# Weight-piece operations with a constant as second input, a later copy of the turned reciprocals, and a new order of the attention stage

## The chip, the cores and the metric

The kernel runs on one core of a Trainium2 chip. The core has TensorE (matrix products, PE in the profile, PEld for its weight loads), VectorE (DVE), ScalarE (ACT), GpSimd (POOL) and SyncE (SP, which here only issues DMA transfers). On-chip memory is SBUF, with 128 partitions, and PSUM, into which TensorE writes.

The metric is the device time of one execution in microseconds. The kernel before took 1176.67 us as the median of three runs (1176.46 to 1177.38).

## The reference

Two stages follow one another: attention with a relative position bias for 8 batches, 8 heads, 576 positions and a head size of 64, and then four dense layers on its 4608 output rows of 512 values.

```python
scores = scale * np.matmul(q, k.transpose(0, 1, 3, 2))
rel = (pos[:, None] - pos[None, :])
psi_rel, psi_i = np.log1p(np.abs(rel)), np.log1p(np.maximum(pos[:, None], 1.0))
h = np.maximum((psi_rel / psi_i)[..., None] @ w1 + b1, 0.0)
scores = scores + (h @ w2).transpose(2, 0, 1)[None]
attn = np.exp(scores - np.max(scores, axis=-1, keepdims=True))
attn = attn / (np.sum(attn, axis=-1, keepdims=True) + 1e-09)
x = np.matmul(attn, v)                        # then heads beside one another: 4608 x 512
a, b = x @ moe_w1, x @ moe_w2                 # 512 -> 1024
out = ((a * b) @ moe_w3) @ moe_w_out          # 1024 -> 1024 -> 512
```

The four weight matrices of the dense layers arrive as 64-bit floats.

## The kernel before

**Four parts.** A prologue computes the bias table from w1, b1 and w2 and writes it to DRAM (`nb_d`). The attention stage works through 32 units. Then the product of w3 and w_out is formed (`fold`) while moe_w1 and moe_w2 are converted, and at last 9 chunks of 512 rows pass the dense layers (`up`, `down`).

**A unit** is a pair of heads (4 pairs) and a batch (8 batches); units are numbered u = 8 x pair + batch. A unit's steps have short names, which the tables use:

- `ldq`, `ldk`, `ldv`: loads of q, k and v. `gq`, `gk`: GpSimd splits q and k into a rounded part (qh, kh, L249) and a residue (ql, kl, L250).
- `S0` to `S7`, `SM`: TensorE's score matmuls for nine tiles of query rows (`M` holds the last 64 rows of both heads), L266. Two PSUM buffers, so a score tile waits until the one before the last has been read.
- `T`: VectorE adds the bias to a score tile and takes the row minimum, L277, with one input in PSUM. `E`: ScalarE takes the exponential and the row sums, L302.
- `F0` to `F3`, `FL`, `FN`: TensorE turns the exponentials, L323 to L335; `H`: the copy of such a turned tile out of PSUM (L346 on VectorE, L348 on ScalarE). `W0`, `W1`: the product with v, L386; `X0`, `X1`: its copy out of PSUM; `xd`: its store to DRAM. F, W and R share two PSUM buffers.
- Once per pair, on its last unit: `r` (VectorE adds 1e-9 to the row sums, L307, and takes reciprocals, L308), `R` (TensorE turns them, L318), `HR` (VectorE copies the turned tile, tile name rt), `rd` (16 small stores on SP's queue).

**Weight pieces.** On six units of each pair (batches 1 to 6) one 128x512 piece of w3 or w_out is converted from 64-bit to 32-bit floats by the function `narrow`, in eight steps `c0` to `c7`: load (SP); magnitude of the upper words (ScalarE, L128); lower words to floats (GpSimd, L134); clamp (VectorE, L137); shift (VectorE, L140); sign and top bit (VectorE, L146); exponent mask (VectorE, L151); a product and a sum (GpSimd, L154 and L155). The same function later converts the pieces of moe_w1 and moe_w2, with the third step on ScalarE.

**The order** is written out by hand. `ORDER` holds for each engine the planned start of each step of a unit; unit u's step has the time u x `PERIOD` + the table's value. `arrange` makes this list, and `drive` issues the instructions on TensorE, ScalarE, VectorE and GpSimd in the order of these times. On each engine instructions run strictly in that order, so only the order that the times make counts on the chip, not the times themselves. A time beyond one period means that the step runs one or two periods after its unit began; taken modulo the period, the times give the cyclic order in the steady state. `AT_R` places R, and HR and rd by offsets to it. The load `c0` is placed 4.4 ahead of the first of c1 and c2. `t_s` (last S or E) and `end` (last step) place the parts behind the attention stage.

Of the kernel before, what the change touches and what calls it, by code (L numbers as in the profile page):

```python
# [9 lines left out]
F32 = mybir.dt.float32  # L10
F32R = mybir.dt.float32r
I32 = mybir.dt.int32
U32 = mybir.dt.uint32
AF = mybir.ActivationFunctionType
ALU = mybir.AluOpType
# [3 lines left out]
P = 128  # L19
# [9 lines left out]
AT_W = 3.5, 0.0, 0.5, 1.2, 2.6, 3.8, 5.5, 7.1, 10.0, 10.6  # L29


PERIOD = 12.49
ORDER = {
    "PE": {
        "S0": 0.00, "S3": 0.41, "S1": 1.76, "S7": 2.29, "S5": 4.20, "S2": 7.21, "SM": 7.62, "S6": 9.04, "F1": 13.82,
        "F0": 15.23, "S4": 15.85, "FL": 21.04, "F2": 25.88, "F3": 28.79, "W0": 29.67, "FN": 32.16, "W1": 34.51,
    },
    "DVE": {
        "T0": 0.71, "T3": 1.40, "T1": 2.43, "T7": 3.12, "T5": 6.30, "T2": 7.88, "c3": 9.03, "c4": 9.54, "TM": 10.13,
        "T6": 10.82, "c5": 11.51, "c6": 12.36, "T4": 18.14, "H3": 29.51, "X0": 32.41, "HN": 33.63, "X1": 37.84,  # L40
    },
    "ACT": {
        "E0": 4.39, "E3": 5.18, "E1": 5.97, "c1": 7.61, "E5": 8.21, "E7": 9.29, "E2": 11.03, "E6": 11.82, "EM": 12.61,
        "H1": 15.02, "H0": 15.97, "E4": 19.29, "HL": 22.61, "H2": 26.60,
    },
    "POOL": {
        "gk": -8.54, "gq": -6.29, "c2": 10.54, "c7": 12.84,
    },
    "SP": {"ldk": -18.63, "ldq": -14.18, "ldv": 0.74},
}  # L50
AT_R = 22.64
TILES = "01234567M"
NPP, NTS, NPS = 7, 4, 2

# [1 line left out]
def arrange(NU, pieces):  # L56

    at = {n: (t, e) for e, steps in ORDER.items() for n, t in steps.items()}
    at.update(r=(max(at["E" + t][0] for t in TILES) + 1.0, "DVE"), R=(AT_R, "PE"), HR=(AT_R + 0.85, "DVE"), rd=(AT_R + 1.3, "SP"))
    at["xd"] = max(t for n, (t, _) in at.items() if n[0] == "X") + 0.8, "SP"  # L60
    at["c0"] = min(at["c1"][0], at["c2"][0]) - 4.4, "SP"
    return {(n, u): (u * PERIOD + t if u or n not in FIRST else FIRST[n], e) for u in range(NU) for n, (t, e) in at.items() if (n[0] != "c" or u in pieces) and (n not in ("r", "R", "HR", "rd") or u % 8 == 7)}


@with_exitstack
def relpos_attention_moe(
# [17 lines left out]
    nc = tc.nc  # L84
# [4 lines left out]
    NTOK, DO = out.shape  # L89
# [7 lines left out]
    def f(ap):  # L97
        return ap.bitcast(F32)

    const = ctx.enter_context(tc.tile_pool(name="const", bufs=1))  # L100
    dram = ctx.enter_context(tc.tile_pool(name="dram", bufs=1, space=DRAM))
    ident = const.tile([P, P], F32, name="ident")
    make_identity(nc, ident)


    WIDE = moe_w1.dtype == mybir.dt.int64
    LEAST = struct.unpack("<f", struct.pack("<I", 0x38000000))[0]
    MOST = struct.unpack("<f", struct.pack("<I", 0x47EFFFFF))[0]

    def narrow(pool, src, n, x, queue, pieces=1, low=nc.scalar):  # L110

        d = {}

        def cut(ap):
            return ap if pieces == 1 else ap.rearrange("p (c n) -> p c n", c=pieces)

        def fetch():
            if not WIDE:
                queue.dma_start(cut(x), src)
                return  # L120
            wi = pool.tile([P, n, 2], I32, name="wi")
            flat = wi.rearrange("p n t -> p (n t)")
            queue.dma_start(cut(flat), src.bitcast(I32))
            mag = pool.tile([P, n], F32, name="wmag")
            d.update(lo=wi[:, :, 0], hi=wi[:, :, 1], mag=mag, bits=mag.bitcast(I32), power=flat[:, 0:n])

        def size():
            nc.scalar.activation(d["mag"], f(d["hi"]), AF.Abs)  # L128

        def rest():  # L130
            if low is nc.scalar:
                nc.scalar.activation(x, d["lo"].bitcast(U32), AF.Copy, scale=2.0 ** -52)
            else:
                low.tensor_scalar(x, d["lo"].bitcast(U32), 2.0 ** -52, 1.0, op0=ALU.mult, op1=ALU.mult)  # L134

        def clamp():
            nc.vector.tensor_scalar(d["mag"], d["mag"], LEAST, MOST, op0=ALU.max, op1=ALU.min)  # L137

        def shift():
            nc.vector.tensor_scalar(  # L140
                d["bits"], d["bits"], 3, 0x3FFFFFFF, op0=ALU.logical_shift_left, op1=ALU.bitwise_and,
            )

        def head():

            nc.vector.scalar_tensor_tensor(  # L146
                d["bits"], d["hi"], -0x40000000, d["bits"], op0=ALU.bitwise_and, op1=ALU.bitwise_or,
            )

        def power():  # L150
            nc.vector.tensor_scalar(d["power"], d["bits"], -0x800000, None, op0=ALU.bitwise_and)  # L151

        def total():
            nc.gpsimd.tensor_tensor(x, x, f(d["power"]), op=ALU.mult)  # L154
            nc.gpsimd.tensor_tensor(x, d["mag"], x, op=ALU.add)  # L155

        steps = [fetch, size, rest, clamp, shift, head, power, total]
        return steps if WIDE else [fetch] + [lambda: None] * 7

# [17 lines left out]
    w3s = [[held.tile([P, DF // 2], F32, name=f"w3s{t}{hf}") for hf in range(2)] for t in range(NF)]  # L177
    wos = [held.tile([P, DO], F32, name=f"wos{t}") for t in range(NF)]
# [14 lines left out]
    cva = att_r.enter_context(tc.tile_pool(name="cva", bufs=1, side="right"))  # L193
# [207 lines left out]

    def piece_of(i):
        if i < NF:
            return narrow(cva, moe_w_out[i * P:(i + 1) * P, :], DO, wos[i], nc.sync, low=nc.gpsimd)
        hf, t = divmod(i - NF, NF)
        return narrow(cva, moe_w3[t * P:(t + 1) * P, hf * 512:(hf + 1) * 512], 512, w3s[t][hf], nc.sync, low=nc.gpsimd)

    pieces = dict(zip([u for u in range(NU) if 0 < u % B < B - 1], (piece_of(i) for i in range(3 * NF))))
    assert len(pieces) == 3 * NF

# [5 lines left out]
    for (n, u), (at, on) in arrange(NU, pieces).items():  # L416
        if n[0] == "H":
            step = lambda n=n, u=u, on=on: op_H(u, n[1:], on)
        elif n[0] == "X":
            step = lambda n=n, u=u, on=on: op_X(u, n[1:], on)  # L420
        else:
            step = lambda n=n, u=u: made[n[0]](u, n[1:])
        later.append((at, len(later), step, n, u))
# [8 lines left out]
    with ExitStack() as pro:  # L432
# [29 lines left out]
        def reach(G):  # L462

            return (G + 1) * GR - 1, S - 1 - G * GR
# [9 lines left out]
        for G in range(NGRP):  # L474
            n = max(reach(G)) + 1
# [49 lines left out]
        for G in range(NGRP):  # L525
            at = -LEAD + G * PACE_B
# [36 lines left out]
    def split_w(pool, t, m):  # L563
        src = (moe_w1, moe_w2)[m].rearrange("(c p) n -> p c n", p=P)[:, :, t * P:(t + 1) * P]
        w = cv.tile([P, NC * P], F32, name="w", bufs=3)
        for step in narrow(cv, src, NC * P, w, nc.sync, pieces=NC):
            step()
            yield
        w = w.rearrange("p (c n) -> p c n", c=NC)
        wh = pool.tile([P, NC, P], F32R, name=f"wh{m}{t}")  # L570
        nc.scalar.activation(wh, w, AF.Copy)
        yield
        wl = pool.tile([P, NC, P], F32R, name=f"wl{m}{t}")
        nc.vector.tensor_tensor(wl, w, f(wh), op=ALU.subtract)  # L574
        ups[m, t] = (wh, wl)
# [142 lines left out]
    for n in range(4, 2 * NF):  # L718
        at = t_s + AT_W1 + PACE_W * n
# [91 lines left out]
```

## Time and profile before

| | |
|---|---|
| median of three runs | 1176.67 us |
| profiled execution, its own time | 1171.91 us |
| profiled execution, span | 1170.1 us |
| busy in the span: TensorE, VectorE, ScalarE, GpSimd | 95%, 55%, 47%, 31% |
| mean granted TensorE clock | 0.987 |
| clamp L137, shift L140, mask L151 (40 of each): busy | 52.3, 34.7, 17.3 us |
| L146 (40): busy | 28.5 us |
| score addition T, L277 (288): busy | 207.5 us |

A profile comes from one execution, which need not lie at the median of the others. Times in the timeline are microseconds from the start of the span. A row of the timeline gives start, length, engine, line, operation, tile written and tiles read, shapes, and in brackets the idle time of the engine before it with what ended it. The attention stage takes roughly the stretch from 72 to 505 us, the dense layers alone that from 632 us on.

### The profile page before, as it was taken

What the parts mean: (1) busy time and instruction counts of PE and PEld (TensorE: products, weight loads), DVE (VectorE), ACT (ScalarE), POOL (GpSimd) and SP (SyncE); (2) the same over time, 40 slices, a digit from 0 to 9 for tenths busy, and PEclk for the clock granted to TensorE, in tenths of its full rate; (3) what the DMA queues carried; (4) which work ended last, traced back from release to release, by engine and by line L of the source; (5) the groups of instructions that cost most, each with busy time, mean ns of one, the idle gap of its engine ahead of it and who ended that gap; (6) DMA issues with size and microseconds to landing.
All of it is one profiled execution on the core that took longest, in us unless ns stands there. A gap on an engine that the chain in (4) does not pass through costs nothing.

```text
span 1170.1 us, 22602 instructions
## 1 busy us (share of the span) xinstructions
PE 1111.9 (95%) x9092; PEld 870.1 (74%) x9092; DVE 647.2 (55%) x1296; ACT 551.9 (47%) x1087; POOL 366.5 (31%) x286
## 2 busy tenths in 40 slices
PE   7669998998999999999999999999999999999998
PEld 3147777777777777766787888888888888888887
DVE  8748878888888788849985322213131322213111
ACT  6667887888888788864343212121211212121211
POOL 0446665775567467525453000000000000000000
PEclk9889999999999999999999999999999999999999
DMA  6864474557454645315341211111110211100001
GB/s 204 271 184 138 154 221 136 170 161 220 130 165 146 209 127 164 108 48 179 130 129 52 75 34 60 48 46 63 37 55 18 79 29 64 45 37 1 36 1 36
DMA packets 61512, 123.14 MB, mean 105 GB/s; under 512 B 9696, under 2 KB 19296, under 8 KB 61408
## 3 DMA queue, kind: packets, MB, share of 16 engines
q1 hardware_dynamic: 60112, 120.21, 32.7%
q10 hardware_dynamic: 1296, 1.49, 0.4%
q8 instruction: 71, 1.16, 0.4%
q14 instruction: 33, 0.27, 0.1%
HBM read 91.76 MB, written 29.92 MB: 104 GB/s over the span
## 4 chain that ended last, share of the span: by engine, by line
PE 51%; DVE 5%; ACT 3%; DMA 3%; POOL 1%; issue 1%; ACTq 0%; SPq 0%; DVEq 0%; POOLq 0%
PE up L653 30%; PE o L678 15%; DMA wi<-in_moe_w_dram 3%; PE pst L386 2%; PE s L266 2%; DVE wmag L137 1%; DVE ts L277 1%; PE pst L323 1%; POOL w L154 1%; PE wacc L611 1%; ACT pp L302 1%; DVE w3l L604 1%; ACT wmag L128 0%; DVE wmag L140 0%; ACT ppM L302 0%
## 5 line engine op out<-in xcount | busy, mean ns | idle before, releaser
L661 DVE TENSOR_TENSOR g<-up,a 128x512 f32<-128x512 f32 x72 | 49.7, 690 | 332.2 <-PE up L653 332.2
L277 DVE CUSTOM_DVE_ANT_0 ts<-s,nb 128x576 f32<-128x576 f32 x288 | 207.5, 753 | 41.8 <-PE s L266 27.2
L653 PE MATMUL up<-xh,wh 128*128 128x512 f32 x576 | 225.2, 391 | 0.5 <-POOL xh L639 0.5
L653 PE MATMUL up<-xh,wl 128*128 128x512 f32 x576 | 225.2, 391 | 0.1
L653 PE MATMUL up<-xl,wh 128*128 128x512 f32 x576 | 225.1, 391 | 0.0
L302 ACT ACTIVATE pp<-ts,mx 128x576 f32<-128x576 f32 x256 | 195.9, 768 | 56.5 <-DVE mx L277 52.0
L678 PE MATMUL o<-w3s,gh 128*128 128x512 f32 x576 | 177.8, 390 | 0.3 <-ACT gh L664 0.3
L386 PE MATMUL pst<-pt,rv 128*64 128x256 f32 (+1 forms) x1280 | 169.2, 410 | 0.2 <-ACT pt L348 0.2
L639 POOL TENSOR_SCALAR xh<-xr 128x512 fp32r<-128x512 f32 x36 | 24.1, 671 | 434.6 <-DVE xr L635 434.6
L658 ACT COPY a<-up 128x512 f32<-128x512 f32 x72 | 42.2, 585 | 246.9 <-PE up L653 246.9
L348 ACT ACTIVATE pt<-pst 128x1024 f32<-128x1024 f32 x128 | 126.3, 1013 | 34.5 <-PE pst L323 34.5
L266 PE MATMUL s<-kh,qh 64*128 64x288 f32 x640 | 119.9, 370 | 22.5 <-DVE mx L277 18.9
L386 PEld LDWEIGHTS pst<-pt,rv 128*64 128x64 f32 x1280 | 88.1, 137 | 62.4 <-issue 11.5
L664 ACT ACTIVATE gh<-g 128x512 fp32r<-128x512 f32 x72 | 45.5, 632 | 174.1 <-DVE g L661 174.1
L653 PEld LDWEIGHTS up<-xh,wh 128*128 128x128 f32 x576 | 108.2, 188 | 24.2 <-POOL xh L639 0.9
L653 PEld LDWEIGHTS up<-xh,wl 128*128 128x128 f32 x576 | 108.2, 188 | 23.9 <-DVE wl L574 0.5
L653 PEld LDWEIGHTS up<-xl,wh 128*128 128x128 f32 x576 | 108.2, 188 | 23.3
L678 PEld LDWEIGHTS o<-w3s,gh 128*128 128x128 f32 x576 | 108.0, 188 | 23.5 <-ACT gh L664 0.7
L323 PE MATMUL pst<-ident,pp 64*128 64x64 f32 x2304 | 104.9, 224 | 11.1 <-ACT ppM L302 10.7
L678 PE MATMUL o<-w3s,gl 128*128 128x512 f32 x288 | 112.2, 390 | 0.9 <-DVE gl L667 0.9
L323 PEld LDWEIGHTS pst<-ident,pp 64*128 64x128 f32 x2304 | 98.0, 140 | 14.6 <-issue 8.4
L266 PE MATMUL s<-kh,ql 64*128 64x288 f32 x640 | 96.6, 295 | 2.4 <-POOL ql L250 2.4
(85 smaller groups left out, 1650.1 us busy)
## 6 DMA issues: line engine op xcount, KB each, us to landing
rq<-in_q_dram SPq DMA_DIRECT2D x31, 640.0 KB
wi<-in_moe_w_dram SPq DMA_DIRECT2D x32, 512.0 KB
nb_d<-bev SPq DMA_DIRECT2D x36, 295.5 KB
rv<-in_v_dram SPq DMA_DIRECT2D x32, 320.0 KB
x_d<-x SPq DMA_DIRECT2D x32, 288.0 KB
xr<-x_d SPq DMA_DIRECT2D x36, 256.0 KB
rb<-r_d SPq DMA_DIRECT2D x72, 128.0 KB
rk<-in_k_dram SPq DMA_DIRECT2D x31, 288.0 KB
```

Source lines behind the costliest of these rows:

```text
L266: nc.tensor.matmul(s[:, hf, :HS], Q[x][rows, q0:q0 + P], K[y][rows, h * HS:(h + 1) * HS], start=(m == 0), stop=(m == len(ops) - 1),)
L277: nc.vector.tensor_tensor_reduce(out=halves(ts), in0=d.pop(("s", t))[:, :, :HS], in1=halves(NB[p, t]), op0=ALU.add, op1=ALU.min, scale=-1. ...
L302: nc.scalar.activation(pp, ts, AF.Exp, bias=mx, scale=-1.0, accum_out=sums[p][:, 9 * b + col:9 * b + col + 1])
L323: nc.tensor.transpose(ps[0:n, hf, c0:c0 + 64], x[rows], ident[rows, rows])
L348: nc.scalar.activation(o, x, AF.Copy)
L386: nc.tensor.matmul(o, x[:, c0:c0 + D], m, start=(c == 0), stop=(c == 4 and n_m == len(ms) - 1),)
L639: nc.gpsimd.tensor_scalar(xh, xr, 1.0, 1.0, op0=ALU.mult, op1=ALU.mult)
L653: nc.tensor.matmul(acc, l[:, cc], r, start=(n == 0), stop=(n == 3 * NC - 1))
L658: nc.scalar.copy(a, ps[0])
L661: nc.vector.tensor_tensor(g, ps[1], a, op=ALU.mult)
L664: nc.scalar.activation(gh, g, AF.Copy)
L678: nc.tensor.matmul(d["o", t], l[:, sl], folded[ft][r], start=(ft == 0 and n == 0), stop=(ft == NF - 1 and n == 2),)
```

## The change

1. `narrow` gets an argument `both`. With `both=False` the clamp becomes a two-input operation whose second input is one column (`least`) repeated along the row, and the same holds for the shift (`low30`) and the exponent mask (`top9`). The pieces of w3 and w_out, that is those of the attention stage, use it; those of moe_w1 and moe_w2 keep the old forms. The three columns are filled once at the start.
2. The copy HR of the turned reciprocals has a time of its own, `AT_HR`, 2.05 behind R instead of 0.85; rd follows it by 0.5.
3. `ORDER` and `PERIOD` are new. X1 moves from VectorE to ScalarE, H3 from VectorE to ScalarE and H0 from ScalarE to VectorE; the steps c1 to c7 now lie one period behind their unit's start, gq comes ahead of gk, and the tiles are taken in another sequence.

```diff
-PERIOD = 12.49
+PERIOD = 12.55
 ORDER = {
     "PE": {
-        "S0": 0.00, "S3": 0.41, "S1": 1.76, "S7": 2.29, "S5": 4.20, "S2": 7.21, "SM": 7.62, "S6": 9.04, "F1": 13.82,
-        "F0": 15.23, "S4": 15.85, "FL": 21.04, "F2": 25.88, "F3": 28.79, "W0": 29.67, "FN": 32.16, "W1": 34.51,
+        "S3": 0.00, "S2": 0.64, "S5": 3.54, "S6": 3.95, "S1": 5.36, "S0": 5.79, "SM": 9.39, "F1": 10.28, "S4": 10.75,
+        "S7": 11.63, "F0": 12.08, "F2": 16.91, "FL": 17.38, "FN": 21.83, "F3": 23.71, "W0": 26.15, "W1": 31.30,
     },
     "DVE": {
-        "T0": 0.71, "T3": 1.40, "T1": 2.43, "T7": 3.12, "T5": 6.30, "T2": 7.88, "c3": 9.03, "c4": 9.54, "TM": 10.13,
-        "T6": 10.82, "c5": 11.51, "c6": 12.36, "T4": 18.14, "H3": 29.51, "X0": 32.41, "HN": 33.63, "X1": 37.84,
+        "T3": 0.67, "T2": 1.36, "T5": 4.21, "T6": 4.90, "T1": 7.08, "T0": 9.29, "TM": 10.54, "T4": 11.42, "T7": 12.30,
+        "H0": 14.60, "c3": 18.14, "c4": 18.91, "c5": 20.32, "c6": 21.12, "HN": 22.53, "X0": 28.89,
     },
     "ACT": {
-        "E0": 4.39, "E3": 5.18, "E1": 5.97, "c1": 7.61, "E5": 8.21, "E7": 9.29, "E2": 11.03, "E6": 11.82, "EM": 12.61,
-        "H1": 15.02, "H0": 15.97, "E4": 19.29, "HL": 22.61, "H2": 26.60,
+        "E3": 2.72, "E2": 3.51, "E5": 6.98, "E6": 7.77, "E1": 8.56, "E0": 10.18, "H1": 11.00, "EM": 12.90,
+        "E4": 13.69, "E7": 14.48, "c1": 16.85, "H2": 17.63, "HL": 18.58, "H3": 24.50, "X1": 34.63,
     },
     "POOL": {
-        "gk": -8.54, "gq": -6.29, "c2": 10.54, "c7": 12.84,
+        "gq": -12.80, "gk": -8.50, "c2": 18.85, "c7": 21.92,
     },
-    "SP": {"ldk": -18.63, "ldq": -14.18, "ldv": 0.74},
+    "SP": {"ldk": -18.65, "ldq": -20.75, "ldv": 0.00},
 }
-AT_R = 22.64
+AT_R, AT_HR = 17.63, 19.68
...
-    at.update(..., R=(AT_R, "PE"), HR=(AT_R + 0.85, "DVE"), rd=(AT_R + 1.3, "SP"))
+    at.update(..., R=(AT_R, "PE"), HR=(AT_HR, "DVE"), rd=(AT_HR + 0.5, "SP"))
...
+    least = const.tile([P, 1], F32, name="least")
+    masks = const.tile([P, 2], I32, name="masks")
+    low30, top9 = masks[:, 0:1], masks[:, 1:2]
+    nc.vector.memset(least, struct.unpack("<f", struct.pack("<I", 0x38000000))[0])
+    nc.vector.memset(low30, 0x3FFFFFFF)
+    nc.vector.memset(top9, -0x800000)
...
         def clamp():
-            nc.vector.tensor_scalar(d["mag"], d["mag"], LEAST, MOST, op0=ALU.max, op1=ALU.min)
+            if both:
+                nc.vector.tensor_scalar(d["mag"], d["mag"], LEAST, MOST, op0=ALU.max, op1=ALU.min)
+            else:
+                nc.vector.scalar_tensor_tensor(d["mag"], d["mag"], MOST, least.broadcast_to([P, n]), op0=ALU.min, op1=ALU.max)
...
+                nc.vector.scalar_tensor_tensor(
+                    d["bits"], d["bits"], 3, low30.broadcast_to([P, n]), op0=ALU.logical_shift_left, op1=ALU.bitwise_and,
+                )
...
+                nc.vector.tensor_tensor(d["power"], d["bits"], top9.broadcast_to([P, n]), op=ALU.bitwise_and)
...
-            return narrow(cva, moe_w_out[i * P:(i + 1) * P, :], DO, wos[i], nc.sync, low=nc.gpsimd)
+            return narrow(cva, moe_w_out[i * P:(i + 1) * P, :], DO, wos[i], nc.sync, low=nc.gpsimd, both=False)
```

More of the change, by code (lines that the diff above doesn't have):

```diff
@@ L58, in arrange @@
     at = {n: (t, e) for e, steps in ORDER.items() for n, t in steps.items()}
-    at.update(r=(max(at["E" + t][0] for t in TILES) + 1.0, "DVE"), R=(AT_R, "PE"), HR=(AT_R + 0.85, "DVE"), rd=(AT_R + 1.3, "SP"))
+    at.update(r=(max(at["E" + t][0] for t in TILES) + 1.0, "DVE"), R=(AT_R, "PE"), HR=(AT_HR, "DVE"), rd=(AT_HR + 0.5, "SP"))
     at["xd"] = max(t for n, (t, _) in at.items() if n[0] == "X") + 0.8, "SP"
@@ L108, in relpos_attention_moe, with narrow @@
     MOST = struct.unpack("<f", struct.pack("<I", 0x47EFFFFF))[0]
-    def narrow(pool, src, n, x, queue, pieces=1, low=nc.scalar):
+    def narrow(pool, src, n, x, queue, pieces=1, low=nc.scalar, both=True):
         d = {}
@@ L136, in clamp @@
         def clamp():
-            nc.vector.tensor_scalar(d["mag"], d["mag"], LEAST, MOST, op0=ALU.max, op1=ALU.min)
+            if both:
+                nc.vector.tensor_scalar(d["mag"], d["mag"], LEAST, MOST, op0=ALU.max, op1=ALU.min)
+            else:
+                nc.vector.scalar_tensor_tensor(d["mag"], d["mag"], MOST, least.broadcast_to([P, n]), op0=ALU.min, op1=ALU.max)
         def shift():
-            nc.vector.tensor_scalar(
-                d["bits"], d["bits"], 3, 0x3FFFFFFF, op0=ALU.logical_shift_left, op1=ALU.bitwise_and,
-            )
+            if both:
+                nc.vector.tensor_scalar(
+                    d["bits"], d["bits"], 3, 0x3FFFFFFF, op0=ALU.logical_shift_left, op1=ALU.bitwise_and,
+                )
+            else:
+                nc.vector.scalar_tensor_tensor(
+                    d["bits"], d["bits"], 3, low30.broadcast_to([P, n]), op0=ALU.logical_shift_left, op1=ALU.bitwise_and,
+                )
         def head():
@@ L150, in power @@
         def power():
-            nc.vector.tensor_scalar(d["power"], d["bits"], -0x800000, None, op0=ALU.bitwise_and)
+            if both:
+                nc.vector.tensor_scalar(d["power"], d["bits"], -0x800000, None, op0=ALU.bitwise_and)
+            else:
+                nc.vector.tensor_tensor(d["power"], d["bits"], top9.broadcast_to([P, n]), op=ALU.bitwise_and)
         def total():
@@ L403, in piece_of @@
         if i < NF:
-            return narrow(cva, moe_w_out[i * P:(i + 1) * P, :], DO, wos[i], nc.sync, low=nc.gpsimd)
+            return narrow(cva, moe_w_out[i * P:(i + 1) * P, :], DO, wos[i], nc.sync, low=nc.gpsimd, both=False)
         hf, t = divmod(i - NF, NF)
-        return narrow(cva, moe_w3[t * P:(t + 1) * P, hf * 512:(hf + 1) * 512], 512, w3s[t][hf], nc.sync, low=nc.gpsimd)
+        return narrow(cva, moe_w3[t * P:(t + 1) * P, hf * 512:(hf + 1) * 512], 512, w3s[t][hf], nc.sync, low=nc.gpsimd, both=False)
     pieces = dict(zip([u for u in range(NU) if 0 < u % B < B - 1], (piece_of(i) for i in range(3 * NF))))
```

## The prediction

> **What bounds the kernel now.** The attention stage runs 32 units (a pair of heads and a batch each) in a periodic order. I read first the busy time of each engine in a stretch of that stage, to see whether one of them is simply full.
>
> ```profile
> core 0: us, PE busy (x) PEld busy (x) DVE busy (x) ACT busy (x) POOL busy (x), PEclk, DMA share, GB/s
> 240.00:280.00 40.00, 38.56 (x553) 29.94 (x553) 34.18 (x81) 33.97 (x70) 28.06 (x20) 1.00 0.58 181
> ```
>
> [...] The timeline of VectorE over one unit says more.
>
> ```profile
> 249.59 0.45 DVE L346 COPY px<-pst 64x64 f32<-64x64 f32 x2
> 250.07 1.45 DVE L137 TENSOR_SCALAR wmag<-wmag 128x512 f32<-128x512 f32 x1
> 251.55 0.82 DVE L140 TENSOR_SCALAR wmag<-wmag 128x512 int32<-128x512 int32 x1
> 252.40 0.76 DVE L277 CUSTOM_DVE_ANT_0 ts<-s,nb 128x576 f32<-128x576 f32 x1
> ...
> 253.08 0.75 DVE L277 CUSTOM_DVE_ANT_0 ts<-s,nb 128x576 f32<-128x576 f32 x1
> ...
> 253.76 0.69 DVE L146 SCALAR_TENSOR_TENSOR wmag<-wi,wmag 128x512 int32<-128x512 int32 x1
> 254.55 0.43 DVE L151 TENSOR_SCALAR wi<-wmag 128x512 int32<-128x512 int32 x1
> ...
> 263.16 0.21 DVE L346 COPY px<-pst 64x64 f32<-64x64 f32 x1
> ```
>
> The px copy comes once per unit: 263.16 - 249.59 = 13.57 us is the period of a unit that carries a weight piece. The clamp (L137) takes 1.45 us and the shift (L140) 0.82. What they take when nothing disturbs them is in the shortest of each line (three numbers: shortest, median, longest, in ns):
>
> ```profile
> L137 DVE TENSOR_SCALAR wmag<-wmag x40: 411/1450/2395, 84.8 to 623.0; 128x512 f32<-128x512 f32 x40
> ...
> L140 DVE TENSOR_SCALAR wmag<-wmag x40: 412/819/1405, 87.2 to 624.0; 128x512 int32<-128x512 int32 x40
> ...
> L146 DVE SCALAR_TENSOR_TENSOR wmag<-wi,wmag x40: 676/686/1186, 89.3 to 626.5; 128x512 int32<-128x512 int32 x40
> ...
> L151 DVE TENSOR_SCALAR wi<-wmag x40: 409/426/834, 90.0 to 627.7; 128x512 int32<-128x512 int32 x40
> ```
>
> So 0.41 us each, and 1.45 us beyond that is a hold. GpSimd's timeline over the same unit shows by what:
>
> ```profile
> 241.48 1.28 POOL L154 TENSOR_TENSOR w3s<-w3s,wi 128x512 f32<-128x512 f32 x1 [2.98 <-DVE wi L151]
> 242.84 1.29 POOL L155 TENSOR_TENSOR w3s<-wmag,w3s 128x512 f32<-128x512 f32 x1
> 244.79 0.67 POOL L249 TENSOR_SCALAR kh<-rk 128x576 fp32r<-128x576 f32 x1 [0.66 <-PE s L266]
> 245.54 1.43 POOL L250 TENSOR_TENSOR kl<-rk,kh 128x576 fp32r<-128x576 f32 x1
> 246.93 1.28 POOL L249 TENSOR_SCALAR qh<-rq 128x1280 fp32r<-128x1280 f32 x1
> 248.29 2.94 POOL L250 TENSOR_TENSOR ql<-rq,qh 128x1280 fp32r<-128x1280 f32 x1
> 251.32 0.77 POOL L134 TENSOR_SCALAR w3s<-wi 128x512 f32<-128x512 uint32 x1
> ```
>
> The clamp was issued at 250.07 while the q residue (ql) ran; ql ended at 251.23 and the clamp 0.29 us later, at 251.52. Then L134 ran to 252.09 and the shift ended 0.28 us after it. The two engines take turns, each for a whole instruction.
>
> Does this hold set the period? The last unit of a pair and the first of the next carry no piece, so their two periods are the comparison:
>
> ```profile
> 167.04 0.21 DVE L346 COPY px<-pst 64x64 f32<-64x64 f32 x1
> ...
> 178.55 2.78 DVE L307 TENSOR_SCALAR sum<-sum 128x72 f32<-128x72 f32 x1
> 181.37 0.60 DVE L308 RECIPROCAL sum<-sum 128x72 f32<-128x72 f32 x1
> 181.89 0.69 DVE L277 CUSTOM_DVE_ANT_0 ts<-s,nb 128x576 f32<-128x576 f32 x1
> ...
> 182.51 0.21 DVE L346 COPY px<-pst 64x64 f32<-64x64 f32 x1
> ...
> 186.47 0.29 DVE L346 COPY rt<-pst 72x128 f32<-72x128 f32 x1 [2.04 <-PE pst L318]
> ...
> 195.27 0.21 DVE L346 COPY px<-pst 64x64 f32<-64x64 f32 x1
> ```
>
> From 167.04 to 182.51 are 15.47 us; the add and the reciprocal of the row sums hold VectorE from 178.55 to 181.89, 3.34 us; without them the bare period is 12.13. A piece therefore costs 13.57 - 12.13 = 1.44 us, which is the 1.45 us of hold: **the period is the bare 12.13 us plus VectorE's wait for GpSimd.**
>
> **The change, part by part.**
>
> *The three forms.* Clamp, shift and exponent mask read a second tile (one column repeated). A free two-input operation here takes 0.69 us (L146) against 0.41: 0.28 more for each of three, 0.83 us of VectorE per piece. The trace of before has no operation with a repeated column, so whether it too is held is unknown. The nearest row has two whole SBUF inputs (GpSimd's row, then VectorE's):
>
> ```profile
> 560.27 1.62 POOL L155 TENSOR_TENSOR w<-wmag,w 128x512 f32<-128x512 f32 x1
> ```
> ```profile
> 560.67 1.78 DVE L635 TENSOR_TENSOR xr<-xr,rb 128x512 f32<-128x512 f32 x1
> ```
>
> GpSimd ended at 561.89, L635 at 562.45: a two-input operation is held as well and ends 0.55 us after GpSimd's, 0.27 later than a one-input one. I take this for the new forms; the other bound is no hold at all. So the forms by themselves lose; what they bring depends on when they meet GpSimd. [...]
>
> *The order.* The table's times modulo 12.55 give each engine's cyclic order. GpSimd: second piece step (c7) at 9.37, gq (qh, ql) at 12.30, gk (kh, kl) at 4.05, c2 at 6.30. VectorE: T5 4.21, T6 4.90, c3 5.59, c4 6.36, T1 7.08, c5 7.77, c6 8.57, T0 9.29. The long ql (by plan 1.0 to 4.0) no longer lies where the clamp is; the shorter kl does (by plan 4.8 to 6.2). c5 and c6 find GpSimd idle, as before. The loop that could bind is c6, c7, gq, gk, c3, c2, c4, T1, c5, c6. From the start-to-start times above: L154 1.36, L155 1.36, qh 1.36, ql 3.03, kh 0.75, kl 1.43, together 9.29 to the end of kl; then c3 0.55, c2 0.57 (252.09 - 251.52), c4 0.55, T1 0.68 (253.08 - 252.40), c5 0.79 (254.55 - 253.76), c6 0.69, and 0.08 to c7: 13.20 us. If GpSimd is late enough for c3 to come before kl starts, c3 goes first and c2 falls behind c4: 9.29 - 1.51 + 0.55 + 1.43 + 0.55 + 2.16 + 0.08 = 12.55. The low bound of the period is the bare 12.13. I take 13.0, nearer to the upper loop because c3 is planned inside kl. Over the periods
>
> ```profile
> 99.29 0.21 DVE L346 COPY px<-pst 64x64 f32<-64x64 f32 x1
> ...
> 497.69 0.21 DVE L346 COPY px<-pst 64x64 f32<-64x64 f32 x1
> ```
>
> there are 29, of which 23 carry a piece: 23 x (13.57 - 13.0) = **-13 us**, bounds -33 (12.13) and, by the last rival, +14.
>
> *X1 to ScalarE, H0 and H3 exchanged.* The copies of H are the same size, so the exchange is worth nothing by itself. X1 (128x320) on ScalarE lies between these two:
>
> ```profile
> L688 ACT COPY osb<-o 128x512 f32<-128x512 f32 x32 | 17.7, 588 | 22.9 <-PE o L678 22.9
> ...
> L693 ACT COPY osb<-o 128x256 f32<-128x256 f32 x4 | 1.5, 373 | 3.4 <-PE o L678 2.9 <-ACT osb L693 0.5
> ```
>
> ScalarE's 33.97 of 40 us is 11.5 per period; with X1 11.9 to 12.1, still under 13.0: nothing, while the cover of a period above 12.1 lasts.
>
> *Reciprocals and their turned copy.* 398.40 us for 29 periods less 23 x 13.57 leaves 86.3 for six bare ones; 6 x 12.13 is 72.8, so three pair ends cost 13.5 us. Two causes: the 3.34 us of reciprocals each (10.0), and HR, which VectorE issues before TensorE has made its turned tile (2.04 us idle). TensorE's own loss behind the reciprocals shows here:
>
> ```profile
> 182.64 0.40 PE L266 MATMUL s<-kh,qh 64*128 64x288 f32 x2 [2.53 <-DVE mx L277]
> ```
>
> After, HR stands 2.05 us behind its transpose instead of 0.85 and T1 lies between: its idle time goes. The add, still a one-input form, comes at 2.93, behind H0, with ql planned until 4.0: I put its hold and work at 2.0 instead of 3.34. R now takes a PSUM tile that H2 frees (planned end 6.03, R at 5.08), up to 0.9 us for TensorE, of which I count half: 2.5 x 3 = 7.5 against 13.5, **-6 us**; bounds 0 and -10. The 16 small stores behind HR still pass through SP's queue, ahead of loads that are due a half period later.
>
> *Ends.* The first expert weight is fetched when the last scores are done:
>
> ```profile
> 503.80 0.38 PE L266 MATMUL s<-kh,qh 64*128 64x288 f32 x2
> ```
> ```profile
> 504.52 0.95 SPq L123 DMA_DIRECT2D wi<-in_moe_w_dram  x2
> ```
>
> The last score tile is S4 at 15.85 before and S7 at 11.63 after, so up to 4.2 us earlier, while unit 31's period now carries a piece: **-2 us**, bounds 0 and -4. The start waits for bias tiles of the last rows at the fourth T in both orders: 0. Three small constant fills on VectorE lie ahead of the first loads: 0. The expert layers keep the old forms.
>
> **Sum.** -13 - 6 - 2 = -21 us on the profiled execution's 1171.9 (span 1170.1), so 1151; the runs shown have a median of 1176.67, 4.8 higher, and on that scale I predict **1155.5**.
>
> **Rivals.**
> First, *no meeting*: a repeated column is not held, or c3 settles ahead of kl and its wait is hidden behind TensorE. For it: T1 is needed only by SM behind W1 at 9.39, over 1.5 us of cover. Against: L635. The period is 12.3, 23 x 1.27 = 29, with 6 and 2: 1139.5.
> Second, *the wait moves*: c3 meets kl and VectorE, 0.83 us fuller, passes nearly all on. Period 13.5: -2, with -6 and -2: 1167.
> Third, *slower: VectorE becomes the bound*. If c3 comes just as kl starts, c3 to the end of c4 takes 1.43 + 1.67 = 3.10 and c5, c6 1.48: 4.58 us, against 2.33 + 1.22 = 3.55 now; less X1's 0.4, VectorE carries 0.6 more per piece, and now every hold reaches the period. Period 14.2: +14, no gain at the pair ends, 1190; with -6 and -2, 1183. It decides from a period of 13.57 + 8/23 = 13.9. Against it: before, c3 to SM has no cover, and after it has.
> Fourth, *nothing*: gains and 0.83 us per piece cancel, 1176.
>
> **How the numbers follow.** Forecast 0.50 (periods 12.7 to 13.3, 1148 to 1162); first rival 0.20; second 0.14; third 0.11; fourth 0.05. The range 1137 to 1175 leaves out the slower case and the outer ends of the first and fourth. About 0.2% (2.4 us) is what a measurement can tell: faster 0.83, same 0.05, slower 0.12.
>
> **What would show it.** The px period between pieces is 12.7 to 13.3. The clamp ends 0.55 us after kl and its median is 1.0 to 1.5 us; the shift ends 0.55 after c2; the mask takes 0.69. The add L307 is shorter than 2.78 us, and the idle time before the rt copy is gone. Wrong if the clamp stays near 0.69 beside a running GpSimd operation (first rival), if the period is above 13.5, or if c3 waits for ql or for ScalarE's magnitude.

## The result, and the profile after

The changed kernel takes 1144.8 us (median of four runs, 1142.36 to 1146.12) against 1177.03 (1176.46 to 1178.1) beside it: a ratio of 0.9723, 95% interval 0.9703 to 0.9743. The predicted time was 1155.5 us, the range 1137 to 1175.

Line numbers have moved: the new clamp is L146, the new shift L154, sign and top bit L160, the new mask L168; GpSimd's lower words are L140, its last two steps L171 and L172; T is L294, the add and the reciprocal L324 and L325, R L335, the copies out of PSUM L363 and L365.

The busy time of each engine, in the same stretch as before:

```profile
core 0: us, PE busy (x) PEld busy (x) DVE busy (x) ACT busy (x) POOL busy (x), PEclk, DMA share, GB/s
240.00:280.00 40.00, 39.59 (x565) 30.78 (x564) 35.01 (x81) 35.42 (x73) 28.47 (x20) 1.00 0.70 221
```

TensorE is busy 39.59 of 40 us instead of 38.56. By itself this does not say that TensorE is the bound: in after_no_clamp_shift, below, it is busy 39.48 of 40 us at a period of 12.70 instead of 12.88.

VectorE's timeline over one unit with a piece:

```profile
254.76 0.45 DVE L363 COPY px<-pst 64x64 f32<-64x64 f32 x2
...
262.79 1.06 DVE L146 SCALAR_TENSOR_TENSOR wmag<-wmag,least 128x512 f32<-128x512 f32 x1
263.88 1.08 DVE L154 SCALAR_TENSOR_TENSOR wmag<-wmag,masks 128x512 int32<-128x512 int32 x1
264.89 0.74 DVE L294 CUSTOM_DVE_ANT_0 ts<-s,nb 128x576 f32<-128x576 f32 x1
265.56 0.68 DVE L160 SCALAR_TENSOR_TENSOR wmag<-wi,wmag 128x512 int32<-128x512 int32 x1
266.35 0.69 DVE L168 TENSOR_TENSOR wi<-wmag,masks 128x512 int32<-128x512 int32 x1
...
267.64 0.45 DVE L363 COPY px<-pst 64x64 f32<-64x64 f32 x2
```

The period is 267.64 - 254.76 = 12.88 us; before it was 13.57. GpSimd over the same unit:

```profile
254.25 1.28 POOL L171 TENSOR_TENSOR w3s<-w3s,wi 128x512 f32<-128x512 f32 x1 [2.71 <-DVE wi L168]
255.61 1.29 POOL L172 TENSOR_TENSOR w3s<-wmag,w3s 128x512 f32<-128x512 f32 x1
256.86 1.27 POOL L266 TENSOR_SCALAR qh<-rq 128x1280 fp32r<-128x1280 f32 x1
258.22 2.92 POOL L267 TENSOR_TENSOR ql<-rq,qh 128x1280 fp32r<-128x1280 f32 x1
261.12 0.67 POOL L266 TENSOR_SCALAR kh<-rk 128x576 fp32r<-128x576 f32 x1
261.87 1.43 POOL L267 TENSOR_TENSOR kl<-rk,kh 128x576 fp32r<-128x576 f32 x1
263.39 1.03 POOL L140 TENSOR_SCALAR w3s<-wi 128x512 f32<-128x512 uint32 x1
267.13 1.29 POOL L171 TENSOR_TENSOR w3s<-w3s,wi 128x512 f32<-128x512 f32 x1 [2.71 <-DVE wi L168]
```

From L171 to L140 GpSimd runs with nothing between; its one gap, 2.71 us, ends with the mask on VectorE. This is the loop that the prediction named. kl ends at 263.30 and the clamp at 263.85, 0.55 us later; L140 ends at 264.42, the shift at 264.96, 0.54 later; T, L160 and L168 follow without a gap, and L171 starts 0.09 after L168.

The end of a pair and the two ends of the stage, VectorE's timeline:

```profile
99.57 0.45 DVE L363 COPY px<-pst 64x64 f32<-64x64 f32 x2
...
273.40 0.70 DVE L324 TENSOR_SCALAR sum<-sum 128x72 f32<-128x72 f32 x1
274.13 0.60 DVE L325 RECIPROCAL sum<-sum 128x72 f32<-128x72 f32 x1
...
277.88 0.28 DVE L363 COPY rt<-pst 72x128 f32<-72x128 f32 x1
...
280.60 0.46 DVE L363 COPY px<-pst 64x64 f32<-64x64 f32 x2 [1.77 <-PE pst L348]
...
293.28 0.46 DVE L363 COPY px<-pst 64x64 f32<-64x64 f32 x2 [2.03 <-PE pst L348]
...
306.86 0.45 DVE L363 COPY px<-pst 64x64 f32<-64x64 f32 x2
...
474.01 0.45 DVE L363 COPY px<-pst 64x64 f32<-64x64 f32 x2
```

From the px copy at 267.64, shown above, the two periods at the end of a pair take 293.28 - 267.64 = 25.64 us; before they took 195.27 - 167.04 = 28.23. The add is down from 2.78 to 0.70 us, and the rt copy waits for nothing.

**Where the time went.** The prediction's stretch of 29 periods goes from the first px copy to the third-last in the kernel before. In the changed kernel the px copies come one period earlier, so the same 29 periods lie between the second copy and the second-last. They take 398.40 us before and 474.01 - 99.57 = 374.44 after: -24.0. Six of them are at pair ends. Before, these take 15.47 + 12.76, 15.50 + 12.78 and 15.47 + 14.44 = 86.4; after, 12.97 + 12.70, 12.96 + 12.68 and 12.94 + 12.68 = 76.9. So **-9.5 us come from the pair ends and -14.5 from the 23 periods with a piece.**

This split hangs on the px copy as the mark. At a pair end the copy waits for TensorE (1.77 and 2.03 us above), with a piece it does not, and the first period with a piece behind each pair end takes 13.58 to 13.59 us (306.86 - 293.28 = 13.58) where the others take about 12.87. With these three times 0.7 us counted to the pair ends, the pair ends give some -7.4 and the pieces -16.6. The last of the 23 periods takes only 12.10 us: GpSimd has no further q and k to split there, and clamp and shift take 0.69 us each.

The spans differ by 1170.1 - 1144.0 = 26.1; the other 2.1 lie outside the 29 periods. These 29 periods are called the stage below. The stage is a finer gauge than whole times, because three executions of the changed kernel have it within 0.6 us (374.44, 374.96, 374.42), while the time at which it begins moves by some microseconds from execution to execution (99.57, 99.34, 97.19; 95.85 and 101.07 in two other executions of kernels with this order).

The dense layers are unchanged: the last weight conversion on GpSimd starts at 629.62 before and at 603.40 after, and from there to the end it is 540.5 and 540.6 us.

### The profile page after: what moved, and what is told of

The parts are those of the page before. It is cut to its first block, busy times and chain, and to the rows that moved or that the text cites. A ratio compares the mean times of both kernels' runs of the same rounds, so it can differ in the third digit from the quotient of the medians.

```text
span 1144.0 us, 22667 instructions
## 1 busy us (share of the span) xinstructions
PE 1103.3 (96%) x9092; PEld 865.1 (76%) x9092; DVE 632.2 (55%) x1267; ACT 564.4 (49%) x1119; POOL 372.0 (33%) x286
## 4 chain that ended last, share of the span: by engine, by line
PE 82%; DMA 3%; ACT 2%; DVE 2%; issue 1%; POOL 1%; SPq 1%; ACTq 0%; DVEq 0%; POOLq 0%
PE up L670 32%; PE o L695 16%; PE pst L403 14%; PE s L283 13%; PE pst L340 6%; DMA wi<-in_moe_w_dram 2%; PE wacc L628 1%; POOL w L171 1%; ACT pt L365 1%; DMA rb<-r_d 1%; PE pst L347 1%; PE pst L351 0%; ACT pp L319 0%; SPq L329 0%; DVE w3l L621 0%
## 5 line engine op out<-in xcount | busy, mean ns | idle before, releaser
L294 DVE CUSTOM_DVE_ANT_0 ts<-s,nb 128x576 f32<-128x576 f32 x288 | 210.6, 754 | 56.5 <-PE s L283 31.7
L365 ACT ACTIVATE pt<-pst 128x1024 f32<-128x1024 f32 x128 | 124.1, 1019 | 23.4 <-PE pst L340 23.4
L340 PE MATMUL pst<-ident,pp 64*128 64x64 f32 x2304 | 102.1, 223 | 0.7 <-ACT pt L365 0.7
```

Of the source, the lines that this page charges most:

```text
L294: nc.vector.tensor_tensor_reduce(out=halves(ts), in0=d.pop(("s", t))[:, :, :HS], in1=halves(NB[p, t]), op0=ALU.add, op1=ALU.min, scale=-1. ...
L340: nc.tensor.transpose(ps[0:n, hf, c0:c0 + 64], x[rows], ident[rows, rows])
L365: nc.scalar.activation(o, x, AF.Copy)
```

## The experiments

Ratios are to the kernel before in the same comparison (medians 1175.0, 1175.2 and 1174.0 us in the three). The stage is that of the profiled execution.

| kernel | period with a piece | stage | median | ratio (95%) |
|---|---|---|---|---|
| before | 13.57 | 398.40 | 1174.0 to 1177.0 | 1 |
| after | 12.87 | 374.44 | 1144.8 | 0.9723 (0.9703 to 0.9743) |
| old_forms_new_order | 12.70 | 371.40 | 1143.15 | 0.9731 (0.9700 to 0.9762) |
| new_forms_old_order | 14.39 | 420.60 | 1195.97 | 1.0177 (1.0148 to 1.0206) |
| before_no_clamp_shift | 12.65 | 378.90 | 1150.79 | 0.9795 (0.9753 to 0.9837) |
| after_no_clamp_shift | 12.70 | 371.51 | 1143.41 | 0.9715 (0.9692 to 0.9739) |
| after_old_hr | 12.87 | 374.36 | 1146.03 | 0.9735 (0.9715 to 0.9755) |
| before_late_hr | 13.57 | 401.95 | 1175.43 | 1.0000 (0.9977 to 1.0022) |
| old_forms_x1_dve | 12.72 | 371.76 | 1146.24 | 0.9734 (0.9714 to 0.9754) |
| before_late_r | 13.57 | 388.52 | 1160.41 | 0.9870 (0.9837 to 0.9902) |
| old_forms_again | 12.70 | 371.50 | 1142.63 | 0.9726 (0.9703 to 0.9749) |
| old_forms_late_r | 12.70 | 370.80 | 1142.04 | 0.9709 (0.9682 to 0.9736) |

The changed kernel itself was run again in the first and third comparison: after_again 1146.02 (0.9751, 0.9723 to 0.9780) and after_third 1144.52 (0.9737, 0.9712 to 0.9761).

### Forms and order taken apart

In *old_forms_new_order* the pieces of w3 and w_out go back to the one-input forms, in the new order:

```diff
-    return narrow(cva, moe_w_out[...], DO, wos[i], nc.sync, low=nc.gpsimd, both=False)
+    return narrow(cva, moe_w_out[...], DO, wos[i], nc.sync, low=nc.gpsimd)
-return narrow(cva, moe_w3[...], 512, w3s[t][hf], nc.sync, low=nc.gpsimd, both=False)
+return narrow(cva, moe_w3[...], 512, w3s[t][hf], nc.sync, low=nc.gpsimd)
```

> The new order and the late HR with the old one-input clamp, shift and mask. Theory 'TensorE binds': the period of 12.87 us is TensorE's own work, the three forms lie under it, so the period stays 12.87 and the time is within 3 us of the changed kernel; the clamp ends 0.29 us after kl. Rival 'the loop through GpSimd and VectorE binds' (13.20 or 12.55 in the prediction): the loop is shorter by 0.27 + 0.27 us, period 12.3 to 12.6, 6 to 13 us faster. Rival 'the forms bring the gain': period above 13.1, 5 us or more slower.

In *new_forms_old_order* the table, `PERIOD`, `AT_R` and the place of HR are those of before, with the two-input forms:

```diff
-PERIOD = 12.55
+PERIOD = 12.49        # and ORDER of before
-AT_R, AT_HR = 17.63, 19.68
+AT_R = 22.64
...
-    HR=(AT_HR, "DVE"), rd=(AT_HR + 0.5, "SP")
+    HR=(AT_R + 0.85, "DVE"), rd=(AT_R + 1.3, "SP")
```

> The old order and the old place of HR with the three two-input forms. Theory 'TensorE binds, the order brings the gain': in the old order the wait for GpSimd reaches the period, and the forms make it longer: clamp and shift each end 0.55 us after GpSimd instead of 0.29, the mask takes 0.26 more, so the period goes from 13.57 to between 14.1 and 14.4, 12 to 19 us slower than before (1189 to 1196). Rival 'the forms bring the gain': faster than before, period 12.9 to 13.3, 1163 or less. If VectorE had room in the old order: 13.57 and 1177.

> The changed kernel once more, beside the next three. All theories: 1145 us within 3, period of a unit with a piece 12.87 us.

The old forms in the new order do not lose the gain, they are 2.9 us faster than the changed kernel beside them, with a stage 3 us shorter (371.40 against 374.4 to 375.0). The new forms in the old order are 21 us slower than before. So **the order brings the whole gain, and the forms by themselves only cost.** In the old order their clamp stands behind ql at every piece (source lines of new_forms_old_order, shortest, median and longest in ns):

```profile
L146 DVE SCALAR_TENSOR_TENSOR wmag<-wmag,least x24: 1711/1725/2670, 84.5 to 506.2; 128x512 f32<-128x512 f32 x24
```
```profile
L154 DVE SCALAR_TENSOR_TENSOR wmag<-wmag,masks x24: 1021/1098/1110, 87.2 to 508.0; 128x512 int32<-128x512 int32 x24
```

1.725 instead of 1.450 and 1.098 instead of 0.819, 0.28 us more each, with the free mask's 0.691 - 0.426 = 0.27: together 0.82, and the period is 14.39 - 13.57 = 0.82 longer. Nothing covers VectorE there, so all three additions reach the period.

Why the old forms are faster in the new order shows in what GpSimd waits for between 200 and 260 us (tile and line, what it waits for, us in total, times, longest). First the changed kernel, then old_forms_again, the repetition of the old forms in the new order:

```profile
POOL w3s L171 <- DVE wi L168: 8.1, 3, 2.7
POOL wos L171 <- DVE wi L168: 5.4, 2, 2.7
```
```profile
POOL w3s L171 <- DVE wi L166: 6.6, 3, 2.2
POOL wos L171 <- DVE wi L166: 4.4, 2, 2.2
POOL qh L266 <- PE s L283: 3.1, 5, 0.7
```

With the new forms the only wait of GpSimd is for the mask, 2.7 us. With the old ones that wait is 2.2, and qh waits up to 0.7 us more for TensorE's score matmuls, which free its buffer: the loop through GpSimd and VectorE now has slack, and the period is 12.70, the same as without clamp and shift (next section).

### Clamp and shift left out

*before_no_clamp_shift* and *after_no_clamp_shift* leave out two steps of the conversion of w3 and w_out, clamp and shift (here the edit of before_no_clamp_shift; the condition `held` is true for these pieces alone):

```diff
-        steps = [fetch, size, rest, clamp, shift, head, power, total]
+        none = lambda: None
+        held = low is nc.gpsimd
+        steps = [fetch, size, rest, none if held else clamp, none if held else shift, head, power, total]
```

> The kernel before with clamp and shift left out of the attention stage's weight pieces (that part of the conversion is missing). The prediction's reading, a bare period of 12.13 us plus 1.44 of wait: period 12.1 to 12.3, 30 to 34 us faster than before. The reading now, that TensorE lost only 2.53 of the 3.34 us of the reciprocals, so that the bare period is 12.9 and 0.7 us of wait reached it: period 12.85 to 13.0, 13 to 17 us faster.

> The changed kernel with clamp and shift left out of the attention stage's weight pieces (that part of the conversion is missing). Theory 'TensorE binds': what its matmuls need in a row is a floor near the 12.65 us that the old order reached without clamp and shift and the 12.70 that the new order reached with the old forms, so the period goes to 12.65 to 12.7, some 4 us faster than the changed kernel, and no further. Rival 'VectorE still sets the period': 2.1 us less work on VectorE, period 12.1 to 12.4, 9 to 15 us faster than the changed kernel.

The old order comes to 12.65 us per period, the new one to 12.70 (VectorE's timeline of before_no_clamp_shift):

```profile
238.75 0.45 DVE L348 COPY px<-pst 64x64 f32<-64x64 f32 x2
...
240.60 1.17 DVE L146 SCALAR_TENSOR_TENSOR wmag<-wi,wmag 128x512 int32<-128x512 int32 x1
...
251.40 0.45 DVE L348 COPY px<-pst 64x64 f32<-64x64 f32 x2
```

These 12.65 to 12.70 us are called the floor below; it is not the 12.13 that the prediction had worked out. In the old order the sign step (L146) now takes 1.17 us instead of 0.69; that it comes beside GpSimd's lower words there is the author's estimate from the order, no row of GpSimd shows it. In after_no_clamp_shift the two VectorE steps that are left take their free 0.69 us each, and the period is no shorter for it. The busy times of after_no_clamp_shift:

```profile
240.00:280.00 40.00, 39.48 (x581) 31.10 (x581) 30.29 (x75) 35.51 (x74) 26.56 (x20) 1.00 0.71 226
```

That the floor is TensorE's work is argued, not shown. VectorE, ScalarE and GpSimd are busy only 30.29, 35.51 and 26.56 of 40 us, and the new order has the same floor with more work on VectorE (12.70 with the old forms) and with less on ScalarE (12.72, X1 back on VectorE, below). But TensorE's 39.48 us don't decide it, for in the changed kernel it is busy 39.59 in longer periods, and no run takes work off TensorE.

So clamp and shift cost 13.57 - 12.65 = 0.92 us per period before, though they took 1.45 + 0.82 = 2.27 us of VectorE; in the changed kernel they cost 12.87 - 12.70 = 0.17 and take 2.14. The measured 12.65 lies between the two readings that were set against each other: 12.13 falls, and 12.9 is too high.

### The place of the copy of the turned reciprocals

*after_old_hr* puts HR back to 0.85 behind R in the new order; *before_late_hr* moves it later in the old one:

```diff
-AT_R, AT_HR = 17.63, 19.68        # after_old_hr
+AT_R, AT_HR = 17.63, 18.48
```
```diff
-HR=(AT_R + 0.85, "DVE"), rd=(AT_R + 1.3, "SP")      # before_late_hr
+HR=(AT_R + 3.30, "DVE"), rd=(AT_R + 3.75, "SP")
```

> The changed kernel with HR 0.85 behind R as before (and rd 0.5 behind HR). The prediction counted the later HR for part of 6 us at the pair ends. Reading of the trace of after: the turned tile is finished at 276.46, VectorE is free from 276.27 and waits for the score tile of T1 until 277.19 anyway, so HR finds a gap there: same time as the changed kernel within 2 us. If the place of HR matters: 2 to 4 us slower, with idle time before the rt copy.

> The kernel before with HR alone moved, from 0.85 to 3.30 behind R, past X1 and T0 (with rd 0.45 behind it). The 2.04 us (3.71 in the third pair) before the rt copy goes. If it was on the path: 2 us per pair end, 5 to 8 us faster than before. If VectorE's wait there is covered, because the period behind it is limited by TensorE: 0 to 2 us.

Neither changes the time: the stage of after_old_hr is 374.36 us against 374.44, and before_late_hr has a ratio of 1.0000. In its profiled execution the stage is 3.6 us longer than in before's: about 0.6 at each pair end, and a second stretch at half clock (last section), 1.7. HR's wait of 2.04 us, which the prediction counted among the causes of the dear pair ends, is idle time of VectorE; taking it away brings nothing.

### X1 back on VectorE

*old_forms_x1_dve* has the old forms and puts the copy X1 back on VectorE:

```diff
     "DVE": { ...
-        ... "HN": 22.53, "X0": 28.89,
+        ... "HN": 22.53, "X0": 28.89, "X1": 34.63,
     "ACT": { ...
-        ... "H3": 24.50, "X1": 34.63,
+        ... "H3": 24.50,
```

> The new order with the old one-input forms and X1 back on VectorE at the same time in the order. TensorE's floor of 12.65 binds: period 12.65 to 12.72, within 2 us of the new order with the old forms (1143). If ScalarE was the limit there, faster by 3 us or more; if VectorE has no room for 0.4 us, slower by 3 us or more.

The period is 12.72 and the stage 371.76 us against 371.40 and 371.50 of the old forms with X1 on ScalarE. The median is 1146.24 against 1143.15 in another comparison, more than the stage can account for. The move costs 0.4 us of stage at most; the rest of the difference is left open.

### The add moved out of the long q residue

*before_late_r* is the old kernel with the add and the reciprocal 3.1 later, behind ql, and R moved behind them; HR and rd stay where they were:

```diff
-r=(max(at["E" + t][0] for t in TILES) + 1.0, "DVE"),
+r=(max(at["E" + t][0] for t in TILES) + 4.11, "DVE"),
-AT_R = 22.64        # HR at AT_R + 0.85, rd at AT_R + 1.3
+AT_R = 23.45        # HR at AT_R + 0.04, rd at AT_R + 0.49
```

> The kernel before with the reciprocals alone moved on VectorE, from ahead of T2 to behind T6 (R then follows them; HR and rd stay where they were). Theory 'the pair ends are the add's wait for ql': the add comes when ql ends, L307 takes 0.2 to 0.9 us instead of 2.8, TensorE's 2.5 us of idle time goes, and with it the stretches of 3.4 us at half clock behind it; each pair end 2 to 4 us shorter, 7 to 12 us faster than before. If the pair ends are limited otherwise: within 3 us of before.

It is 13.6 us faster than the kernel before. The period with a piece is unchanged at 13.57, the stage 9.9 us shorter. VectorE's timeline and GpSimd's of before_late_r:

```profile
184.05 0.19 DVE L307 TENSOR_SCALAR sum<-sum 128x72 f32<-128x72 f32 x1
184.28 0.60 DVE L308 RECIPROCAL sum<-sum 128x72 f32<-128x72 f32 x1
...
186.30 0.28 DVE L346 COPY rt<-pst 72x128 f32<-72x128 f32 x1 [1.42 <-PE pst L318]
```
```profile
180.93 2.95 POOL L250 TENSOR_TENSOR ql<-rq,qh 128x1280 fp32r<-128x1280 f32 x1
```

ql ends at 183.88; the add comes at 184.05 and takes 0.19 us instead of 2.78. HR still waits 1.42 us, and it does no harm. So **what makes the old pair ends dear is that the add waits for nearly the whole of ql**. Without the 1.67 us of before's half-clock stretch (last section), which this kernel doesn't have, the stage is 8.2 us shorter, 2.7 per pair end. In the new order the pair ends gain 2.6 each by the same px marks, or 1.9 with the longer period behind them counted in. The 13.6 us by the medians are more than the 7 to 12 that were expected; the stage shows 9.9 of them.

### The old forms again, and R behind two score tiles

At a pair end of the changed kernel R takes a PSUM tile that H2 (L365) must free. The chain of waits (start, length, what) has H2 with its whole length of 1.04 us, but TensorE stands still for less: by its own timeline it turns tiles until 275.78 and waits 0.38 us.

```profile
275.07 1.04 ACT pt L365
...
276.15 0.30 PE pst L335
```
```profile
275.55 0.23 PE L340 MATMUL pst<-ident,pp 64*128 64x64 f32 x2
276.15 0.30 PE L335 MATMUL pst<-ident,sum 128*72 128x128 f32 x1 [0.38 <-ACT pt L365]
```

It is the only wait that the trace lists for TensorE from 100 to 474 us: 0.37 to 0.39 us at each of the three pair ends.

*old_forms_again* repeats the old forms beside the changed kernel (after_third); *old_forms_late_r* adds to them an R that comes behind S1 and S0:

```diff
-AT_R, AT_HR = 17.63, 19.68
+AT_R, AT_HR = 18.74, 19.68
```

> The changed kernel once more, for comparison beside the next two: 1145 us within 2, period 12.87 us.

> The new order with the old one-input forms, again: period 12.70, 3 us faster than the changed kernel beside it (19 periods by 0.17). If the first result was scatter: equal within 1 us.

> As the run before, with R moved behind S1 and S0 (to 18.74), just ahead of W1. In the changed kernel TensorE stands about 1 us at R until ScalarE's H2 has freed a PSUM tile; with the two score tiles ahead of it 0.85 us of that is filled. Theory: pair ends shorter by 0.5 to 0.9 us each, 1.5 to 2.7 us faster than the new order with the old forms. If W1 then waits for HL instead: no difference.

The old forms take 1142.63 us (1142.12 to 1143.96), the changed kernel 1144.52 (1142.55 to 1145.64): 1.9 by the medians where 3 were expected, 2.9 by the stage (371.50 against 374.42). The periods with a piece are shorter. The first period of a pair end is longer (13.78 us against 12.96), but the period behind the pair end is shorter in turn (12.74 against 13.58): the same 0.7 us falls on another side of the px copy. **The old forms in the new order are the better kernel of the two**, by about 0.2%.

With R later, the stage is 370.80, another 0.7 us, and the period at the pair end is 13.46 instead of 13.78 us (VectorE's timelines of old_forms_late_r and old_forms_again):

```profile
261.86 0.45 DVE L363 COPY px<-pst 64x64 f32<-64x64 f32 x2
...
275.32 0.46 DVE L363 COPY px<-pst 64x64 f32<-64x64 f32 x2 [2.15 <-PE pst L348]
```
```profile
267.30 0.46 DVE L363 COPY px<-pst 64x64 f32<-64x64 f32 x2
...
281.08 0.46 DVE L363 COPY px<-pst 64x64 f32<-64x64 f32 x2 [1.77 <-PE pst L348]
```

The expectation counted on about 1 us of standing at R in the changed kernel; TensorE's wait there is 0.37 to 0.39 us, as above. In old_forms_late_r its timeline has no wait at R (271.87), and 0.2 to 0.3 us per pair end come back. In whole times, 1142.04 (1137.79 to 1143.24) against 1142.63, it can't be told from nothing.

## Why the prediction was right or wrong

**The period: right in its loop, 0.3 too long in its terms.** The prediction's upper loop was c7, gq, gk, c3, c2, c4, T1, c5, c6 at 13.20 us, and it took 13.0. The rows above show just this loop: 9.05 from L171 to the end of kl, then 0.55, 0.57, 0.54, 0.60, 0.79, 0.69 and 0.09, together 12.88. The prediction had 9.29 for the first term, because it took its lengths start to start from rows of before in which GpSimd stood in another sequence; here L172 to qh is 1.25 instead of 1.36 and ql to kh 2.90 instead of 3.03. Its T1 was 0.08 too long. Its reason for 13.0, a point between two loops, was not a mechanism: the period is the upper loop, with c3 inside kl, and the lower loop does not occur. That 13.0 came so near is in part luck: leaning towards a loop that doesn't occur made up for lengths that were 0.3 too long. The first rival needed 12.3, which the floor of 12.65 to 12.70 excludes.

Over the 23 periods with a piece the term was -13; measured were -14.5, of which the last period alone gives 1.5 (12.10 us against 13.58).

**A column that is repeated is held: right.** The clamp ends 0.55 us after kl and the shift 0.54 after L140, as the row of L635 had it, with medians well above the free 0.69 (source lines of the changed kernel):

```profile
L146 DVE SCALAR_TENSOR_TENSOR wmag<-wmag,least x24: 686/1070/1119, 95.1 to 469.9; 128x512 f32<-128x512 f32 x24
```
```profile
L154 DVE SCALAR_TENSOR_TENSOR wmag<-wmag,masks x24: 691/1071/1111, 96.2 to 470.7; 128x512 int32<-128x512 int32 x24
```

The clamp's median is 1.07, at the lower edge of the 1.0 to 1.5 that was given.

**"The bare 12.13 us plus VectorE's wait": wrong.** The bare period was worked out by taking VectorE's whole 3.34 us from the period at a pair end, though the prediction's own row shows TensorE losing only 2.53 there. With 2.53 it is 15.47 - 2.53 = 12.94, already above the floor of 12.65 to 12.70 that both kernels without clamp and shift show. The run that moves the add alone gives the rest: in before_late_r this period is 12.62, so the place of the add and the reciprocal cost 15.47 - 12.62 = 2.85 us of it. The equality of 1.44 us of cost and 1.45 us of clamp was a coincidence: clamp and shift together cost 0.92. This is why the periods below 12.6, the lower bound and the first rival's 29 us were never to be had.

**Reciprocals and HR: the place right, one of the two causes wrong.** The term was -6, bounds 0 and -10; measured were -9.5 by the px marks, or -7.4 with the longer periods behind the pair ends. The add and the reciprocal, put at 2.0 us, take 0.70 and 0.60. As the prediction had it, the add still meets ql, but only its end: it comes at 273.40, ql ends at 271.10 + 2.94 = 274.04, and the add 0.06 later (GpSimd's row).

```profile
271.10 2.94 POOL L267 TENSOR_TENSOR ql<-rq,qh 128x1280 fp32r<-128x1280 f32 x1
```

HR's idle time, given as the second cause, cost nothing (after_old_hr, before_late_hr). R's wait on H2 was put at up to 0.9, of which half was counted, and TensorE waits 0.38. And 1.7 of the gain is an effect that the prediction did not know of, told in the last section: before's third pair end is longer than the other two by 14.44 - 12.77 = 1.67 us. The rest, 7.8 or 5.7, is 2.6 or 1.9 per pair end.

**Ends: right in sum.** The term was -2; 2.1 lie outside the 29 periods. Its first step holds: the first expert weight is fetched 476.61 - 474.01 = 2.60 us behind the end of the stage instead of 504.52 - 497.69 = 6.83, so 4.2 earlier (SyncE's queue, and GpSimd's last step of the last weight, in the changed kernel).

```profile
476.61 1.71 SPq L129 DMA_DIRECT2D wi<-in_moe_w_dram  x2
```
```profile
603.40 1.29 POOL L172 TENSOR_TENSOR w<-wmag,w 128x512 f32<-128x512 f32 x1
```

From there to that last step are 126.8 us, where before they were 629.62 - 504.52 = 125.1, so 1.7 are given back. Why the conversions there take longer was not looked into.

**The scale.** By the profiled executions the change is 1171.9 - 1145.8 = 26.1 us against the predicted 21; by the medians it is 32.2 in the first comparison and 29 in the two later ones in which the kernel ran again. The prediction added 4.8 us, the distance of before's profiled execution from its median, to both kernels. The changed kernel's profiled execution lies 1.0 above its median instead. So some half of the miss of 10.7 us is in the sum and the other half in this shift. The period of 12.87 lies in the 12.7 to 13.3 of the forecast, the time of 1144.8 below its 1148 to 1162. The time at which the stage begins differs by up to 5 us between executions, and the profiled executions of the old order have between none and three stretches at half clock (last section); how the 4.8 us divide between these is open.

**The third rival**, VectorE as the bound with a period of 14.2, has its like only where the order was left alone: new_forms_old_order has 14.39 and 1195.97 us, though there the clamp stands behind ql and not at the start of kl. In the new order VectorE's steps from c3 to c6 are part of the loop of 12.88.

## What to carry to other kernels

Where two engines take turns, choose by the loop, not by one instruction's length: follow the operations in a circle, add up their rows, and compare the sum with the period that is left when the operations in question are taken out; below that floor a shorter operation bought nothing here (12.70 us with the old forms as without clamp and shift). A short operation that comes while a long one of the contending engine runs can cost the long one's rest (here 2.78 us for an add that takes 0.19 behind it), so moving it behind the long one's end can be worth more than any other form of it (here -13.6 us for an add and a reciprocal that are issued four times). And before a change with several parts is kept, each part wants its own run: here the order brought everything, and the new forms that came with it cost 2 to 3 us.

## What the runs showed of the hardware

**TensorE's granted clock fell to 0.51 for 3.5 us behind one of three waits of 2.5 us.** In the kernel before, the third pair end is 1.67 us longer than the others. The first view gives the busy times of two stretches there, with the columns of the table at the top; the second is TensorE's timeline of the same place, and the last row is the product W1 of the first pair end:

```profile
403.50:407.00 3.50, 3.50 (x20) 1.82 (x16) 0.24 (x2) 1.63 (x4) 0.00 (x0) 0.51 0.08 28
407.00:408.00 1.00, 1.00 (x16) 0.81 (x15) 0.55 (x2) 0.00 (x0) 0.00 (x0) 1.00 0.00 0
```
```profile
401.95 0.40 PE L266 MATMUL s<-kh,qh 64*128 64x288 f32 x2 [2.52 <-DVE mx L277]
...
402.55 4.50 PE L386 MATMUL pst<-pt,rv 128*64 128x320 f32 x20
```
```profile
183.23 2.85 PE L386 MATMUL pst<-pt,rv 128*64 128x320 f32 x20
```

The granted clock (third value from the end) is 0.51 and then 1.00 again; the same 20 products take 4.50 us instead of 2.85. All three pair ends of before had nearly the same wait ahead of them, 2.53, 2.55 and 2.52 us, and the clock fell at the third alone. In new_forms_old_order all three pair ends show it, at 0.50, 0.51 and 0.50; the first of them:

```profile
188.40:191.80 3.40, 3.40 (x16) 1.63 (x14) 0.42 (x2) 1.63 (x4) 0.00 (x0) 0.50 0.17 61
```

In before_no_clamp_shift and before_late_hr two of three show it, at 0.50. In the changed kernel the granted clock is 1.00 in every microsecond from 100 to 480 us, and TensorE waits 0.37 to 0.39 us at its pair ends. In before_late_r TensorE's timeline has no wait at the first pair end, the 20 products of W1 take 2.86 us there, and the three pair ends take 25.4 to 25.5 us (px marks, with 13.57 for the periods with a piece between them), none 1.67 longer than another. What decides whether a wait of 2.5 us is followed by such a stretch was not shown.

**The turns hold GpSimd as well.** L140 takes 1.03 us behind the new clamp, against 0.77 before behind the old one (medians of w3's 16 pieces 1.019 and 0.772). In both it ends 0.57 us after the clamp (264.42 - 263.85 and 252.09 - 251.52): with the longer clamp on VectorE GpSimd's operation took 0.26 us more, so here the new form's extra length was paid on both engines.
